# Gated mix of a spectral and a dense branch: output product 7 split a second time, product 3 on one couple less, some sums and partial results by DMA

## The chip, the core and the metric

The kernel runs on one core of a Trainium2 chip. The metric is the device time of one execution in microseconds (us). A core has five engines that each work through a queue of their own, in a fixed order: TensorE (PE in the profile; PEld is its weight load), VectorE (DVE), ScalarE (ACT), GpSimd (POOL) and SyncE (SP). Data move between DRAM and the on-chip buffer (SBUF) by DMA; matmuls write into PSUM banks.

## The reference

```python
# x 2048x1024, h 2048x3584, out 2048x1024, all fp32
a = x @ dft_hid_re.T ; b = x @ dft_hid_im.T
A = dft_seq_re @ a - dft_seq_im @ b          # real part of a 2-D DFT
h = relu(x @ w1 + b1) ** 2
B = h @ w2 + b2
g = sigmoid((x * gate_w).sum(-1, keepdims=True))
out = g * A + (1 - g) * B
```

## The kernel before

Nearly all the work is four big matrix products, in five parts. Part x makes a and b (the hidden DFT) and leaves them in DRAM as `ab`. Parts a and b make h from the first 2048 and the last 1536 columns of w1, and leave it in DRAM. Part c is the sequence DFT (with -Ci beside Cr its K is a and b together) and leaves the gated spectral branch in DRAM. Part o is h times w2, gated and added to that, and writes the output. The products of x, a and b are interleaved (constant `ORDER`); c and o follow, each in the order 1, 2, 5, 6, 3, 7, 4 of their products.

**Seven products.** A big product is split in 2 x 2 quarters and computed by seven products instead of eight (`FACTORS`): product p multiplies a quarter, or a sum of quarters, of the left side (S1 to S4) with one of the right side (T1 to T4), and the results are added up to the four quarters of the output. The class `Seven` (L422) keeps the partial results that several products share ("one", "u", "s", "v"). Those that the table `SPILL` names for a part are stored to DRAM (`keep`, L448) and, for the uses listed, read back by `get` (L458); the others stay in SBUF.

**A second level.** Inside a product the same is done once more where it is told to. For c and o (function `tall`, L617) K stands in 8 and 7 blocks, taken in couples of two. `TWICE_C` and `TWICE_O` say for each product how many couples are split into seven inner products; what is left of K is multiplied at one level. A couple takes 84 matmuls at two levels and 96 at one. A matmul has 128x128 weights and 512 columns (L1425).

**fp32 from three terms.** Each operand is split in a rounded part hi (ScalarE, L203, or L407 for a half-size one) and the rest lo (VectorE, L211 or L209, half-size L418 or L415); TensorE multiplies hi by hi, hi by lo and lo by hi. A half-size operand (256 columns) holds hi and lo in one tile, `both`. So every operand of every inner product costs ScalarE and VectorE a pass, and every sum of blocks one more (L182 at full size, L388 at half size), unless it is made by DMA.

**Sums by DMA.** `Side` (L333) makes the sums S and T of blocks. A sum that `BY_DMA` names for its side (`x_r` is the right side of part x, `o_r` of part o, and so on) isn't added on VectorE: SP loads one block, and POOL issues a DMA that adds the other to it (`accumulate`, L169). Plain loads are issued by SP, stores and adding DMAs by POOL.

**Inside a product at two levels** (`tall.product`). Inner products 1 and 6 share a group of PSUM banks, where `CHAIN` says so: 1 is emptied by ScalarE (`put`, L308: acc<-ps), 6 is then added on top. ScalarE empties also 5; VectorE adds (L321: acc+ps, L329: acc+acc) these to the four results so far. The second half, inner products 2, 3 and 4, starts from banks into which ScalarE loads a partial result (L255: ps<-acc). Which one that is, `LATE` decides:

```python
674:  late = old and p in LATE[name] and not ends
678:  f01, f11 = (both(old[b], f, 4, 0) if old and not late else f for b in (b01, b11))
680:  n01 = both(f01, t, 4, 0)
682:  n10 = both(old[b10], t, 4, 0) if old and not late else t
685:  onto = old if late else parts
686:  groups = {2: Group(2, [k2 + more], [onto[b00]]), 3: Group(2, [k2 + more], [onto[b01]]),
```

`old` is what the products before have left for the same quarter of the output. With `late` the banks are loaded with it, and the product's own inner results (`parts`) are added by VectorE when the second half is done; without, `old` and the inner results are first added on VectorE, and their sum is what the banks are loaded with. A finished quarter of part o is gated on VectorE (L960), the last ones row by row (L989).

**The order of the queues.** The kernel has a planner that runs when it is built: it holds a list of all operations with costs and due times, and plays them through to set a static order of each engine's queue, a slot of SBUF for each tile (55 slots) and a pair of PSUM banks for each group (4 pairs). `EARLY` puts the first sums of some sides ahead of time; `GUARD` bounds how far an engine may take work from further down while an operation of a PSUM bank is about to be ready (L1350, L1353); `DISTANT` holds operations back that are needed only much later, when few slots are free (L1358). So a change of one table can change the order on any engine.

Of the kernel before, what the change touches and what calls it, by code (L numbers as in the profile page):

```python
# [25 lines left out]
DMA_END = 2.2  # L26
GRID = 2.0

ORDER = (("ab", 1), ("x", 1), ("x", 2), ("b", 2), ("a", 2), ("b", 6), ("a", 6), ("x", 6), ("a", 5), ("b", 5), ("x",
         5), ("a", 3), ("x", 3), ("b", 3), ("a", 7), ("x", 7), ("b", 7), ("x", 4), ("a", 4), ("b", 4), ("c", 0), ("o",  # L30
         0))
ORDER_C = (1, 2, 5, 6, 3, 7, 4)
# [1 line left out]
INNER = {"x": (1, 5, 6, 3, 7, 2, 4), "a": (1, 5, 6, 3, 7, 2, 4), "b": (1, 5, 6, 3, 7, 2, 4)}  # L34
TWICE_X = (1, 2, 4, 5, 6, 7, 3)
TWICE_HA = (2, 3, 4, 5, 6, 7, 1)
TWICE_HB = (2, 3, 4, 5, 6, 7, 1)
TWICE_C = {1: 4, 2: 3, 3: 4, 4: 3, 6: 3, 5: 3}
TWICE_O = {1: 3, 2: 3, 3: 3, 4: 3, 6: 3}

FACTORS = {1: ((0, 0), (0, 0)), 2: ((0, 1), (1, 0)), 3: ("S4", (1, 1)), 4: ((1, 1), "T4"), 5: ("S1", "T1"),
           6: ("S2", "T2"), 7: ("S3", "T3")}
# [18 lines left out]
MIX_R = {"T1": ((0, 0), (0, 1), ADD), "T2": ((1, 1), "T1", SUB), "T3": ((0, 1), (1, 1), SUB),  # L61
         "T4": ("T2", (1, 0), ADD)}
LESS_X, LESS_H, LESS_C, LESS_O = (3, 4), (3, 4, 5), (2, 6), (3, 4, 5)
BY_DMA = {"x_l": ("S1", "S2", "S3", "S4"), "x_r": ("T4",), "h_l": ("S4",), "c_l": ("S1", "S2", "S3", "S4"), "c_r":
          ("T1", "T2", "T3", "T4"), "o_l": ("S3", "S4"), "o_r": ("T2", "T4")}

AHEAD = {"SP": 15.0, "POOL": 15.0, "ACT": 15.0, "DVE": 15.0}
FILL = {"DMA": 1.05, "ACT": 0.97, "DVE": 0.97}
# [4 lines left out]
KEEP = 5  # L73
EAGER = True
WARM = 38
LATE = {"c": (1, 2, 3, 4, 5, 6, 7), "o": (1, 2, 3, 4, 5, 6)}
DISTANT = (15.0, 6)
SPILL = {"one": ("", "x"), "u": ("xb", "ab"), "s": ("x", "xb"), "v": ("", "b")}
CHAIN = {"c": {1: 1, 2: 1, 3: 1, 4: 1, 5: 2, 6: 1, 7: 1}, "o": {3: 1, 1: 1, 2: 1, 4: 1, 6: 1, 7: 1}}
SUMMED = "xab"  # L80
ADD_S = ""
ADD_U = "bx"
EARLY = {"a_l": (("S2", "S1"), (), 90.0, 7.5), "b_l": (("S2",), (), 75.0, 15.0), "x_r": (("T1",), (), 60.0, 7.5)}
TOGETHER = True
OPEN = True
REST = 1.0
GUARD = (0.5, 1.0)
SOON = {"POOL": 12.0, "ACT": 6.0, "DVE": 6.0}
SLACK = {"SP": 3.0, "POOL": 2.0, "ACT": 0.6, "DVE": 0.6}
LEAD = {"SP": 3.0, "POOL": 1.0, "ACT": 2.0, "DVE": 2.0}  # L90
# [2 lines left out]
C_FORMS = ()  # L93
O_FORMS = ()
THROUGH_X = ("S1", "S2")
THROUGH_H = ("S2",)
THROUGH_W = ()
THROUGH_C = ("T2",)
THROUGH_O = ("T2",)
# [3 lines left out]
def gated_mix_kernel(ctx: ExitStack, tc: tile.TileContext, x4, xn, w4, ct, w1a, w1b, w2, b1, b2, gw, out):  # L103
# [201 lines left out]
    def put(group, seg, rp, scale=1.0, name="acc"):  # L305
        w, rows = Val(name), group.rows
        c, l = act(512 * min(2, rows - 2 * rp))
        group.take(seg, rp, Op("ACT", c, l, [], w, lambda: nc.scalar.activation(  # L308
            view(w.tile, rows, rp), view(group.ps[rp], rows, rp), AF.Copy, scale=scale)))
        return w  # L310
# [111 lines left out]
    class Seven:  # L422
# [97 lines left out]
    def wide(name, left, right, rows, second, less, final, from_ps, negative, flip, place=None):  # L520
# [13 lines left out]
        def product(p, old, quad):  # L534
# [37 lines left out]
            chain, other = Group(rows, [1] * 4), Group(rows, [1] * 2)  # L572
            opening = OPEN and name in ORDER[0][0] and p == (ALIKE[ORDER[0][1]] if name == "x" else ORDER[0][1])
            if opening:
# [42 lines left out]
    def tall(name, left, right, ksteps, order, second, less, final, from_ps, by_row=None):  # L617
# [4 lines left out]
        def product(p, old, quad):  # L622
# [26 lines left out]
            def block(q, j, c):  # L649
                if isinstance(r, str):  # L650
                    if (q, j, c) not in raw:
                        raw[q, j, c] = right[2 * q + j, c].of(r)
                    return raw[q, j, c]
                return right[2 * q + j, c].of(r)

            r2 = {q: Inner(lambda j, c, q=q: block(q, j, c), INNER_R) for q in range(k2)}
            chain = min(CHAIN[name].get(p, 0), k2)
            groups = {p2: Group(2, [k2]) for p2 in (1, 6, 7, 5) if p2 != 1 or not chain}
# [14 lines left out]
            ends = by_row and p == order[-1]  # L673
            late = old and p in LATE[name] and not ends
            t = put(g1, 0, 0)
# [97 lines left out]
    def order_of(run):  # L773
        return [ALIKE[p] if run == "x" and TOGETHER else p for r, p in ORDER if run in r]

    NEG = ((0, 1), (1, 0))

    def x_stage():
# [12 lines left out]
        def x_block(m, q):  # L791
            return lambda *k: Far(x4[2 * k[0] + m, k[1], q], 0.0) if len(k) > 1 else sum_of_x(m, q, k[0])

        keep = None if TOGETHER else lambda s, v, m, q: x_sums.__setitem__((m, q, s), (v, len(steps)))
        left = x_sides
        left.update({(m, q): Side(x_block(m, q), PLUS_L, BY_DMA["x_l"],
                                  keep=keep and (lambda s, v, m=m, q=q: keep(s, v, m, q)), through=THROUGH_X,
                                  made=had("x_l", (m, q)))
                     for m in range(2) for q in range(2)})
        right = {(q, c): Side(lambda j, n, q=q, c=c: Far(w4[n, c, j, q], 0.0), MIX_R, BY_DMA["x_r"], through=THROUGH_W,  # L800
                              made=had("x_r", (q, c)))
# [10 lines left out]
    def h_stage(part):  # L812
# [35 lines left out]
        def from_ps(quad, k, group, seg, rp):  # L848
            end(quad, k, None, lambda: group.ps[rp], lambda o: group.take(seg, rp, o))

        left = {(m, q): Side(lambda i, j, m=m, q=q: Far(w1[i, m, j, q], 0.0), MIX_L, BY_DMA["h_l"], rows * P,
                             through=THROUGH_H, made=had("ab"[part] + "_l", (m, q)))
                for m in range(2) for q in range(2)}
        names = {"T1": "S3", "T2": "S2", "T3": "S1", "T4": "S4"}

        def blocks(q, c):
            def get(*key):
                if len(key) == 1:
                    return sum_of_x(c, q, names[key[0]])
                j, n = key  # L860
                return Far(x4[2 * n + c, j, q], 0.0)
            return get
# [10 lines left out]
        right = {(q, c): Same(q, c) if TOGETHER else Side(blocks(q, c), None, ()) for q in range(2) for c in range(2)}  # L873
        return wide("ab"[part], left, right, rows, TWICE_HB if part else TWICE_HA, LESS_H, final, from_ps, False, True)

# [42 lines left out]
    def c_stage():  # L918
        rows = [Late(lambda n=n: row(n, 0, 1e9)) for n in range(2)]

        def end(quad, k, v, source, take=None):
# [14 lines left out]
            if take:  # L936
                take(o)
            store(gy[i, n, c, rp], w)

        left = {q: Side(lambda i, j, q=q: ab[j, q, i], PLUS_L, BY_DMA["c_l"], through=THROUGH_C,  # L940
                        made={f: c_forms[f, q] for f in C_FORMS}) for q in range(8)}
        right = {(q, c): Side(lambda j, n, q=q, c=c: Far(ct[n, c, j, q], 0.0), PLUS_R, BY_DMA["c_r"], through=THROUGH_C, made=had("c_r", (q, c)))
                 for q in range(8) for c in range(2)}
# [12 lines left out]
    def o_stage():  # L956
# [5 lines left out]
        def end(quad, k, v, source, take=None):  # L962
            (i, n), (c, rp) = quad, k
            r, y = rows[n, -1 if quad in NEG else 1].of(), gy[i, n, c, rp]
            w = Val("o")
            cc, l = dve(512)

            def first():
                for j in range(2):
                    begin(w.tile[:, j, :], source()[:, j, :], r.tile[:, c, :], 4 * i + 2 * rp + j, quad)  # L970

            o = Op("DVE", 2 * cc, cc + l, ([v] if v else []) + [r, b2v], w, first, over=[v] if v else [])
            o.soon = True
            if take:
                take(o)
            Op("POOL", 0.6, 2 * P * 4 * 512 * 2, [w, y], Far(y.at), lambda: nc.gpsimd.dma_start(y.at, w.tile, accum_op=ADD)
               ).twice = True

        def by_row(quad, k, group):
            (i, n), (c, rp) = quad, k  # L980
            r, y = rows[n, -1 if quad in NEG else 1].of(), load(gy[i, n, c, rp])
            for j in range(2):
# [3 lines left out]
                def emit(w=w, j=j):  # L986
# [7 lines left out]

        left = {q: Side(lambda i, j, q=q: Far(w2[i, j, q], 0.0), MIX_L, BY_DMA["o_l"], through=THROUGH_O, made=had("o_l", q)) for q in range(7)}
        right = {(q, c): Side(lambda j, n, q=q, c=c: h_far[j, q, 2 * n + c], PLUS_R, BY_DMA["o_r"], through=THROUGH_O,
                             made={f: o_forms[f, q, c] for f in O_FORMS})
                 for q in range(7) for c in range(2)}
        tall("o", left, right, 7, ORDER_O, TWICE_O, LESS_O, lambda quad, k, v: end(quad, k, v, lambda: v.tile),
             lambda quad, k, group, seg, rp: end(quad, k, None, lambda: group.ps[rp], lambda o: group.take(seg, rp, o)),  # L1000
# [4 lines left out]
    def sums_early():  # L1005
# [320 lines left out]
    def try_engine(e, now):  # L1326
# [6 lines left out]
        for o in queue:  # L1333
# [225 lines left out]
```

## Time and profile before

| | us |
|---|---|
| median of 3 runs | 1793.14 (1793.13 to 1793.51) |
| profiled execution, its own time | 1793.0 |
| span of the profile | 1791.1 |
| TensorE busy | 1785.1 (100%) |
| VectorE busy | 1621.8 (91%) |
| ScalarE busy | 1007.6 (56%) |
| GpSimd busy | 288.9 (16%) |

The parts follow one another in time: x, a and b from 5.4 to 738.5 us, c to 1293.4, o to the end. Part o's products 1, 2, 5, 6, 3, 7 and 4 end at 1361, 1429, 1506, 1574, 1642, 1718 and 1786 us. Times of matmuls start at the row's first number; TensorE is pipelined, so the time from start to start, and not a matmul's own length, is what one costs. Rows name instructions as out<-in with the kernel's names; "x2" means that the row stands for two of them, one behind the other. In brackets stands the idle time ahead of an instruction and what ended it.

### The profile page before, as it was taken

What the parts mean: (1) busy time and instruction counts of PE and PEld (TensorE: products, weight loads), DVE (VectorE), ACT (ScalarE), POOL (GpSimd) and SP (SyncE); (2) the same over time, 40 slices, a digit from 0 to 9 for tenths busy, and PEclk for the clock granted to TensorE, in tenths of its full rate; (3) what the DMA queues carried; (4) which work ended last, traced back from release to release, by engine and by line L of the source; (5) the groups of instructions that cost most, each with busy time, mean ns of one, the idle gap of its engine ahead of it and who ended that gap; (6) DMA issues with size and microseconds to landing.
All of it is one profiled execution on the core that took longest, in us unless ns stands there. A gap on an engine that the chain in (4) does not pass through costs nothing.

```text
span 1791.1 us, 21814 instructions
## 1 busy us (share of the span) xinstructions
PE 1785.1 (100%) x7892; PEld 1477.9 (83%) x7892; DVE 1621.8 (91%) x1671; ACT 1007.6 (56%) x1201; POOL 288.9 (16%) x416
## 2 busy tenths in 40 slices
PE   9999999999999999999999999999999999999998
PEld 8888888888888888888888888888888888888887
DVE  8896899999898897999998999559999998999887
ACT  7454743324669576866574747336476435754443
POOL 0113211011211222001133201202000031101020
PEclk9999999999999999999999999999999999999999
DMA  8959898898979999789899959999675997789992
GB/s 328 390 217 301 279 359 271 302 339 258 286 278 342 301 302 333 249 301 305 229 238 269 253 167 304 302 282 283 222 258 188 374 278 206 223 273 331 297 226 59
DMA packets 145531, 492.73 MB, mean 275 GB/s; under 512 B 15872, under 2 KB 29520, under 8 KB 145424
## 3 DMA queue, kind: packets, MB, share of 16 engines
q0 software_dynamic: 58064, 207.13, 44.2%
q1 hardware_dynamic: 86656, 283.04, 43.3%
q8 instruction: 62, 1.02, 0.2%
q10 hardware_dynamic: 704, 1.18, 0.2%
q14 instruction: 45, 0.37, 0.1%
HBM read 377.51 MB, written 113.78 MB: 274 GB/s over the span
## 4 chain that ended last, share of the span: by engine, by line
PE 99%; DMA 0%; DVE 0%; ACT 0%; issue 0%
PE ps L1425 99%; DMA raw<-in_x 0%; DVE o L960 0%; DVE o L989 0%; ACT hi L1464 0%
## 5 line engine op out<-in xcount | busy, mean ns | idle before, releaser
L1425 PE MATMUL ps<-hi 128*128 128x512 f32 x1638 | 635.9, 389 | 0.1
L1425 PE MATMUL ps<-hi,lo 128*128 128x512 f32 x1638 | 635.9, 389 | 0.0
L1425 PE MATMUL ps<-lo,hi 128*128 128x512 f32 x1638 | 635.7, 389 | 0.0
L1425 PE MATMUL ps<-hi,both 128*128 128x512 f32 x1960 | 605.2, 389 | 0.0
L203 ACT ACTIVATE hi<-raw 128x1024 fp32r<-128x1024 f32 (+1 forms) x326 | 333.2, 1038 | 269.5 <-DVE raw L182 183.1
L1425 PEld LDWEIGHTS ps<-hi,both 128*128 128x128 f32 x1960 | 367.9, 188 | 76.4
L211 DVE TENSOR_TENSOR lo<-raw,hi 128x1024 fp32r<-128x1024 f32 (+1 forms) x291 | 346.9, 1204 | 39.0 <-ACT hi L203 38.5
L1425 PE MATMUL ps<-lo,both 128*128 128x512 f32 x980 | 381.2, 389 | 0.0
L1425 PEld LDWEIGHTS ps<-hi,lo 128*128 128x128 f32 x1638 | 307.4, 188 | 64.3 <-DVE lo L211 0.4
L1425 PEld LDWEIGHTS ps<-hi 128*128 128x128 f32 x1638 | 307.4, 188 | 64.1 <-ACT hi L1464 0.4
L1425 PEld LDWEIGHTS ps<-lo,hi 128*128 128x128 f32 x1638 | 307.4, 188 | 63.9
L203 ACT ACTIVATE hi<-sum 128x1024 fp32r<-128x1024 f32 (+1 forms) x217 | 220.7, 1028 | 138.5 <-DVE sum L182 113.4
L211 DVE TENSOR_TENSOR lo<-sum,hi 128x1024 fp32r<-128x1024 f32 (+1 forms) x183 | 218.7, 1199 | 19.2 <-ACT hi L203 11.6
L321 DVE TENSOR_TENSOR acc<-acc,ps 128x1024 f32<-128x1024 f32 (+1 forms) x165 | 187.8, 1142 | 44.9 <-PE ps L1425 38.9
L1425 PEld LDWEIGHTS ps<-lo,both 128*128 128x128 f32 x980 | 183.9, 188 | 38.2
L308 ACT ACTIVATE acc<-ps 128x1024 f32<-128x1024 f32 (+1 forms) x135 | 132.9, 987 | 143.8 <-PE ps L1425 139.6
L182 DVE TENSOR_TENSOR raw<-raw 128x1024 f32<-128x1024 f32 (+1 forms) x146 | 168.3, 1173 | 0.0
L203 ACT ACTIVATE both<-sum 128x512 fp32r<-128x512 f32 x140 | 87.1, 624 | 86.5 <-DVE sum L388 59.0
L255 ACT ACTIVATE ps<-acc 128x1024 f32<-128x1024 f32 (+1 forms) x83 | 81.2, 980 | 73.6 <-DVE acc L321 66.4
L321 DVE TENSOR_TENSOR back<-back,ps 128x1024 f32<-128x1024 f32 x64 | 71.8, 1126 | 15.0 <-PE ps L1425 14.3
L407 ACT ACTIVATE both<-raw 128x512 fp32r<-128x512 f32 x105 | 64.7, 618 | 26.9 <-PE ps L1425 15.7
L182 DVE TENSOR_TENSOR sum<-sum 128x1024 f32<-128x1024 f32 (+1 forms) x56 | 65.6, 1181 | 9.6 <-DMA sum<-in_ct 6.3
(68 smaller groups left out, 1133.8 us busy)
## 6 DMA issues: line engine op xcount, KB each, us to landing
raw<-h SPq DMA_DIRECT2D x107, 512.0 KB, 6.3
raw<-in_ct SPq DMA_DIRECT2D x91, 512.0 KB, 7.6
raw<-in_w SPq DMA_DIRECT2D x81, 512.0 KB, 7.2
back<-v SPq DMA_DIRECT2D x48, 512.0 KB, 6.6
raw<-in_ct POOLq DMA_DIRECT2D x48, 512.0 KB, 12.3
raw<-ab SPq DMA_DIRECT2D x40, 512.0 KB, 11.3
t<-raw POOLq DMA_DIRECT2D x38, 512.0 KB, 12.2
sum<-t SPq DMA_DIRECT2D x38, 512.0 KB, 14.6
```

The costliest lines, as they stand in the source:

```text
L182: Op("DVE", c, l, [a, b], w, lambda: nc.vector.tensor_tensor(w.ap(), a.ap(), b.ap(), op=op), over=[a, b])
L203: nc.scalar.activation(self.hi()[:, k, :], src(v)[:, k, :], AF.Copy, scale=-1.0 if less else 1.0)
L211: nc.vector.tensor_tensor(a, b, c, op=SUB)
L255: lambda rp=rp, k=k, e=e, v=v: nc.scalar.activation(self.ps[rp][:, :k, :], v.tile[:, e:e + k, :], AF.Copy),
L308: group.take(seg, rp, Op("ACT", c, l, [], w, lambda: nc.scalar.activation(view(w.tile, rows, rp), view(group.ps[rp], rows, rp), AF.Copy, s ...
L321: nc.vector.tensor_tensor(a, b, d, op=ADD)
L407: Op("ACT", c, l, [v.base], hi, lambda: nc.scalar.activation(self.hi(), cols(v), AF.Copy, scale=-1.0 if less else 1.0), then=lambda t: set ...
L1425: nc.tensor.matmul(group.ps[r // group.per][:, r % group.per, :], a()[:, kk, r * P:(r + 1) * P], b()[:, kk, :], start=first and kk + n == ...
```

## The change

Only tables of the kernel change; no function is edited.

- Output product 7 is computed at two levels on three couples of K (it was at one level throughout), product 3 on two couples instead of three. `CHAIN` gets an entry for product 5 of o, which has no couple at two levels.
- The sums T1 of part x's right side (4 tiles) and T3 of part o's right side (14 tiles) are made by adding DMAs.
- `LATE` of part o loses 3 and 6. Product 7, now at two levels, is not in it either.
- `SPILL`: x's "one" is no longer stored and read back; the list of u has part a's first use in it, besides those of x and b, so all three parts read u back.
- Numbers of the planner: `ORDER` has a6 ahead of b6, `EARLY` and `GUARD` have other values, `DISTANT` holds nothing back any more. `THROUGH_H` and `TWICE_HB` alter no instruction.

```diff
-... ("b", 2), ("a", 2), ("b", 6), ("a", 6), ("x", 6), ...
+... ("b", 2), ("a", 2), ("a", 6), ("b", 6), ("x", 6), ...
-TWICE_HB = (2, 3, 4, 5, 6, 7, 1)
+TWICE_HB = (2, 4, 5, 6, 7, 1, 3)
 TWICE_C = {1: 4, 2: 3, 3: 4, 4: 3, 6: 3, 5: 3}
-TWICE_O = {1: 3, 2: 3, 3: 3, 4: 3, 6: 3}
+TWICE_O = {1: 3, 2: 3, 3: 2, 4: 3, 6: 3, 7: 3}
...
-BY_DMA = {... "x_r": ("T4",), ... "o_l": ("S3", "S4"), "o_r": ("T2", "T4")}
+BY_DMA = {... "x_r": ("T1", "T4"), ... "o_l": ("S3", "S4"), "o_r": ("T2", "T3", "T4")}
...
-LATE = {"c": (1, 2, 3, 4, 5, 6, 7), "o": (1, 2, 3, 4, 5, 6)}
-DISTANT = (15.0, 6)
-SPILL = {"one": ("", "x"), "u": ("xb", "ab"), "s": ("x", "xb"), "v": ("", "b")}
-CHAIN = {... "o": {3: 1, 1: 1, 2: 1, 4: 1, 6: 1, 7: 1}}
+LATE = {"c": (1, 2, 3, 4, 5, 6, 7), "o": (1, 2, 4, 5)}
+DISTANT = (1000.0, 0)
+SPILL = {"u": ("xab", "ab"), "s": ("x", "xb"), "v": ("", "b")}
+CHAIN = {... "o": {3: 1, 1: 1, 2: 1, 4: 1, 6: 1, 7: 1, 5: 1}}
...
-EARLY = {"a_l": (("S2", "S1"), (), 90.0, 7.5), ... "x_r": (("T1",), (), 60.0, 7.5)}
+EARLY = {"a_l": (("S2", "S1"), (), 70.0, 7.5), ... "x_r": (("T1",), (), 40.0, 7.5)}
...
-GUARD = (0.5, 1.0)
+GUARD = (0.7, 3.0)
```

The program has 7830 matmuls in its matrix products after the change, 7854 before; VectorE issues 25 instructions more, ScalarE 23 more, POOL 426 DMAs instead of 420, SP 547 instead of 562. At three places the new order of the queues is shown, with the numbers that tell tiles of one name apart.

**VectorE in product 4 of part x**, up to the lo that TensorE multiplies with at matmul 50 of that product. raw and sum are blocks and their sums, acc and back are partial results (back: one that was read back from DRAM), ps is a bank of PSUM. Before:

```order
L182 TENSOR_TENSOR raw_5109<-raw_5324,raw_5109 128x1024
L329 TENSOR_TENSOR back_5331<-back_5331,acc_5398 128x512
L321 TENSOR_TENSOR acc_5119<-acc_5119,ps_5377 128x1024
L321 TENSOR_TENSOR acc_5152<-acc_5152,ps_5400 128x1024
L209 SCALAR_TENSOR_TENSOR lo_5488<-sum_5407,hi_5442 128x1024
L329 TENSOR_TENSOR back_5361<-back_5361,acc_5413 128x1024
L182 TENSOR_TENSOR sum_5496<-sum_5288,sum_5401 128x1024
L211 TENSOR_TENSOR lo_5500<-sum_5401,hi_5409 128x1024
```

After:

```order
L182 TENSOR_TENSOR raw_5063<-raw_5296,raw_5063 128x1024
L329 TENSOR_TENSOR back_5322<-back_5322,acc_5391 128x512
L321 TENSOR_TENSOR acc_5110<-acc_5110,ps_5369 128x1024
L182 TENSOR_TENSOR sum_5449<-sum_5249,sum_5396 128x1024
L209 SCALAR_TENSOR_TENSOR lo_5477<-sum_5389,hi_5398 128x1024
L329 TENSOR_TENSOR back_5327<-back_5327,acc_5402 128x1024
L321 TENSOR_TENSOR acc_5145<-acc_5145,ps_5393 128x1024
L211 TENSOR_TENSOR lo_5492<-sum_5396,hi_5431 128x1024
```

The second addition out of PSUM (L321) and the sum of blocks (L182) have changed places.

**ScalarE in product 6 of part o**, from the row that empties a bank of inner product 1 to the second bank that is loaded. Before:

```order
L308 ACTIVATE acc_12736<-ps_12413 128x1024
L255 ACTIVATE ps_12713<-acc_11327 128x1024
L203 ACTIVATE hi_12744<-sum_12470 128x1024
L203 ACTIVATE hi_12760<-raw_11937 128x1024
L407 ACTIVATE both_12763<-raw_11946 128x2x256
L255 ACTIVATE ps_12738<-acc_11305 128x1024
```

After:

```order
L308 ACTIVATE acc_12742<-ps_12419 128x1024
L203 ACTIVATE both_12747<-sum_12415 128x2x256
L203 ACTIVATE hi_12764<-sum_12412 128x1024
L203 ACTIVATE hi_12767<-raw_11910 128x1024
L255 ACTIVATE ps_12720<-acc_11325 128x1024
L407 ACTIVATE both_12778<-raw_11942 128x2x256
L203 ACTIVATE hi_12793<-raw_11951 128x1024
L203 ACTIVATE both_12798<-sum_12506 128x2x256
L255 ACTIVATE ps_12744<-acc_11302 128x1024
```

The loads of the banks have moved back, behind three splits of operands (hi and both). In product 7, which had no second level before, **VectorE** now has these rows around the end of inner product 6; the acc on the left are the four results:

```order
L329 TENSOR_TENSOR acc_13042<-acc_13042,acc_13883 128x1024
L329 TENSOR_TENSOR acc_13072<-acc_13072,acc_13883 128x1024
L329 TENSOR_TENSOR acc_13042<-acc_13042,acc_13906 128x1024
L211 TENSOR_TENSOR both_13868<-sum_13559,both_13868 128x2x256
L321 TENSOR_TENSOR acc_13906<-acc_13906,ps_13620 128x1024
L211 TENSOR_TENSOR lo_13936<-sum_13538,hi_13888 128x1024
L329 TENSOR_TENSOR acc_13020<-acc_13020,acc_13906 128x1024
```

What the rows make are the sums that the banks of inner products 2, 3 and 4 are loaded with.

**ScalarE early in product 4 of part o**, up to the row that empties inner product 1's bank. Before:

```order
L203 ACTIVATE hi_14190<-sum_13837 128x1024
L203 ACTIVATE hi_14206<-sum_14188 128x1024
L203 ACTIVATE both_14214<-sum_14121 128x2x256
L203 ACTIVATE both_14232<-sum_14228 128x2x256
L308 ACTIVATE acc_14249<-ps_14118 128x1024
```

After:

```order
L203 ACTIVATE both_14231<-sum_14207 128x2x256
L203 ACTIVATE hi_14237<-sum_14186 128x1024
L203 ACTIVATE both_14271<-sum_14255 128x2x256
L203 ACTIVATE hi_14275<-sum_13813 128x1024
L308 ACTIVATE acc_14290<-ps_14163 128x1024
```

A full-size hi now stands just ahead of that row, where a half-size one stood.

More of the change, by code (lines that the diff above doesn't have):

```diff
@@ L27 @@
 GRID = 2.0
-ORDER = (("ab", 1), ("x", 1), ("x", 2), ("b", 2), ("a", 2), ("b", 6), ("a", 6), ("x", 6), ("a", 5), ("b", 5), ("x",
+ORDER = (("ab", 1), ("x", 1), ("x", 2), ("b", 2), ("a", 2), ("a", 6), ("b", 6), ("x", 6), ("a", 5), ("b", 5), ("x",
          5), ("a", 3), ("x", 3), ("b", 3), ("a", 7), ("x", 7), ("b", 7), ("x", 4), ("a", 4), ("b", 4), ("c", 0), ("o",
@@ L63 @@
 LESS_X, LESS_H, LESS_C, LESS_O = (3, 4), (3, 4, 5), (2, 6), (3, 4, 5)
-BY_DMA = {"x_l": ("S1", "S2", "S3", "S4"), "x_r": ("T4",), "h_l": ("S4",), "c_l": ("S1", "S2", "S3", "S4"), "c_r":
-          ("T1", "T2", "T3", "T4"), "o_l": ("S3", "S4"), "o_r": ("T2", "T4")}
+BY_DMA = {"x_l": ("S1", "S2", "S3", "S4"), "x_r": ("T1", "T4"), "h_l": ("S4",), "c_l": ("S1", "S2", "S3", "S4"),
+          "c_r": ("T1", "T2", "T3", "T4"), "o_l": ("S3", "S4"), "o_r": ("T2", "T3", "T4")}
 AHEAD = {"SP": 15.0, "POOL": 15.0, "ACT": 15.0, "DVE": 15.0}
@@ L75 @@
 WARM = 38
-LATE = {"c": (1, 2, 3, 4, 5, 6, 7), "o": (1, 2, 3, 4, 5, 6)}
-DISTANT = (15.0, 6)
-SPILL = {"one": ("", "x"), "u": ("xb", "ab"), "s": ("x", "xb"), "v": ("", "b")}
-CHAIN = {"c": {1: 1, 2: 1, 3: 1, 4: 1, 5: 2, 6: 1, 7: 1}, "o": {3: 1, 1: 1, 2: 1, 4: 1, 6: 1, 7: 1}}
+LATE = {"c": (1, 2, 3, 4, 5, 6, 7), "o": (1, 2, 4, 5)}
+DISTANT = (1000.0, 0)
+SPILL = {"u": ("xab", "ab"), "s": ("x", "xb"), "v": ("", "b")}
+CHAIN = {"c": {1: 1, 2: 1, 3: 1, 4: 1, 5: 2, 6: 1, 7: 1}, "o": {3: 1, 1: 1, 2: 1, 4: 1, 6: 1, 7: 1, 5: 1}}
 SUMMED = "xab"
@@ L82 @@
 ADD_U = "bx"
-EARLY = {"a_l": (("S2", "S1"), (), 90.0, 7.5), "b_l": (("S2",), (), 75.0, 15.0), "x_r": (("T1",), (), 60.0, 7.5)}
+EARLY = {"a_l": (("S2", "S1"), (), 70.0, 7.5), "b_l": (("S2",), (), 75.0, 15.0), "x_r": (("T1",), (), 40.0, 7.5)}
 TOGETHER = True
@@ L95 @@
 THROUGH_X = ("S1", "S2")
-THROUGH_H = ("S2",)
+THROUGH_H = ()
 THROUGH_W = ()
```

## The prediction

> **What bounds the kernel now.** I read the page's parts 1 and 2, then the chain of waits in order of time, then the timeline where TensorE stops, then the busy time product by product.
>
> ```profile
> span 1791.1 us, 21814 instructions
> PE 1785.1 (100%) x7892; PEld 1477.9 (83%) x7892; DVE 1621.8 (91%) x1671; ACT 1007.6 (56%) x1201; POOL 288.9 (16%) x416
> PEclk9999999999999999999999999999999999999999
> ...
> 5.42 1779.48 PE ps L1425 x7848
> ...
> 1784.93 0.76 DVE o L960
> ...
> 1787.10 0.69 DVE o L989
> ```
>
> TensorE works from 5.42 us to the end at its full clock; 5.4 us stand ahead of it and 6 behind, which no edit touches. 1779.48 us for 7848 matmuls are 226.7 ns each, start to start. The matmul groups of the page add up to 7854 (three of 1638, one of 1960, one of 980), so a whole stall of TensorE has room for about 0.3 us. It is in one place, 50 matmuls into x4 (product 4 of part x):
>
> ```profile
> 645.00 0.39 PE L1425 MATMUL ps<-lo,hi 128*128 128x512 f32 x1
> 645.35 0.50 PE L1425 MATMUL ps<-hi,lo 128*128 128x512 f32 x1
> 645.68 0.40 PE L1425 MATMUL ps<-hi 128*128 128x512 f32 x1
> ...
> 645.35 0.19 PEld L1425 LDWEIGHTS ps<-hi,lo 128*128 128x128 f32 x1 [0.39 <-DVE lo L211]
> ...
> 639.53 1.22 DVE L321 TENSOR_TENSOR acc<-acc,ps 128x1024 f32<-128x1024 f32 x1 [0.26 <-PE ps L1425]
> ...
> 644.08 1.22 DVE L211 TENSOR_TENSOR lo<-sum,hi 128x1024 fp32r<-128x1024 f32 x1
> ```
>
> Starts are 0.35 and 0.33 apart where 0.227 is normal: 0.12 waited for VectorE's lo (ended 645.30) and 0.11 to get going again, 0.23 in all. So every matmul counts in full, and VectorE, with hardly a gap of its own, is the next bound. By product of part o:
>
> ```profile
> core 0: us, PE busy (x) PEld busy (x) DVE busy (x) ACT busy (x) POOL busy (x), PEclk, DMA share, GB/s
> 1293.00:1361.00 68.00, 68.00 (x302) 56.31 (x301) 67.90 (x76) 44.22 (x54) 1.62 (x3) 1.00 0.59 209
> 1506.00:1574.00 68.00, 68.00 (x302) 56.31 (x301) 67.26 (x74) 45.30 (x56) 7.40 (x10) 1.00 0.60 172
> 1642.00:1718.00 76.00, 76.00 (x337) 62.94 (x336) 60.46 (x63) 32.21 (x35) 14.28 (x17) 1.00 1.01 281
> 1718.00:1786.00 68.00, 68.00 (x302) 56.17 (x300) 60.26 (x69) 33.07 (x40) 8.67 (x10) 1.00 0.58 121
> ```
>
> These are products 1, 6, 7 and 4. Two levels on three couples leave VectorE 0.1 to 0.7 us of 68 (products 1 and 6); product 7 at one level leaves 15.5 of 76, but there the DMA share is 1.01.
>
> **The change part by part.**
>
> *TWICE_O.* A couple of K takes 84 matmuls at two levels, 96 at one. Product 7 gains three couples, product 3 loses one: 24 matmuls less, 24 x 0.2267 = **-5.44 us**, all on the path. VectorE pays: the changed program has 43 full-size (1024) and 33 half-size instructions between product 7's first and last matmul, against 43 and 19. At the steps of the rows below (1.135 and 0.60 us from start to start) that is 68.6 us in a window of 68.0. It is product 1's load (67.90, no stall) and a little more; what covers it is the lead built up in product 3, which loses such work. I take 0 for throughput; the cover lacking entirely would be the 0.6.
>
> *The stall in x4.* VectorE's order ahead of that lo is shown with the change (the lo is the last row of both fences there). The same rows, but the second read of PSUM, which waited 0.26 us for TensorE, now stands three rows later, when its bank has long been ready. A stall of 0.12 goes with the 0.26: **-0.23 us**.
>
> *LATE without 3 and 6, and product 7 as it is built.* These now add the old partial result before the second half of the product: a bank is loaded (ScalarE, L255) only after VectorE's sum. The second pair of fences with the change shows product 6. Before, the load followed the emptying of the chain's bank at once; now it waits for VectorE's sums; the fence behind them shows how these are queued in product 7. The bank that its last row is loaded into is used 36 matmuls (8.16 us) after the end of inner product 6. Product 1, which has no old result, shows the nearest such chain and its prices:
>
> ```profile
> 1328.90 0.62 PE L1425 MATMUL ps<-hi,both 128*128 128x512 f32 x2
> ...
> 1323.89 1.03 ACT L308 ACTIVATE acc<-ps 128x1024 f32<-128x1024 f32 x1 [0.23 <-PE ps L1425]
> ...
> 1326.80 1.03 ACT L255 ACTIVATE ps<-acc 128x1024 f32<-128x1024 f32 x1
> 1328.19 1.03 ACT L255 ACTIVATE ps<-acc 128x1024 f32<-128x1024 f32 x1 [0.36 <-DVE acc L321]
> ...
> 1324.42 1.21 DVE L211 TENSOR_TENSOR lo<-raw,hi 128x1024 fp32r<-128x1024 f32 x1
> 1325.56 1.21 DVE L329 TENSOR_TENSOR acc<-acc 128x1024 f32<-128x1024 f32 x1
> 1326.87 1.22 DVE L321 TENSOR_TENSOR acc<-acc,ps 128x1024 f32<-128x1024 f32 x1
> 1328.01 0.68 DVE L418 TENSOR_TENSOR both<-raw,both 128x512 fp32r<-128x512 f32 x1
> 1328.61 1.22 DVE L182 TENSOR_TENSOR raw<-raw,sum 128x1024 f32<-128x1024 f32 x1
> ```
>
> There the first load ended at 1327.83, 1.30 us before its matmul (1329.13, the second of the first row). In product 7: three sums at 1.135, the half-size 0.60, two rows at 1.135, the last sum 1.22, 0.1 to hand over, the load 1.03 = 8.6 us, 0.46 late if the first sum begins just as inner product 6 ends. In product 6 a lo stands among the sums instead: 5.76 against 5.44 us (24 matmuls) for the first bank and again 8.6 against 8.16 for the second, 0.46 in all. Where in its row VectorE stands at that moment the order doesn't tell: half a row (0.57) either way gives 0 to 1.0 for each. I take 0.3 for each, nearer to the start on time; product 3 (two couples, 24 matmuls for a shorter chain) costs 0.
>
> *Behind product 7.* Its four results are added and gated on VectorE while product 4 starts. By the last pair of fences with the change, a hi that waits for VectorE's sum now stands just ahead of the row that empties inner product 1's bank, and TensorE needs that bank 12 matmuls (2.72 us) later. Prices:
>
> ```profile
> 1726.45 1.03 ACT L308 ACTIVATE acc<-ps 128x1024 f32<-128x1024 f32 x1 [0.77 <-PE ps L1425]
> 1727.50 1.06 ACT L203 ACTIVATE hi<-sum 128x1024 fp32r<-128x1024 f32 x1
> ...
> 1724.32 0.69 DVE L388 TENSOR_TENSOR sum<-raw 128x512 f32<-128x512 f32 x1
> 1724.93 1.41 DVE L960 SCALAR_TENSOR_TENSOR acc<-acc,b2c,g 128x512 f32<-128x512 f32 x2
> 1726.25 1.22 DVE L182 TENSOR_TENSOR sum<-sum 128x1024 f32<-128x1024 f32 x1
> ...
> 1728.74 0.61 PE L1425 MATMUL ps<-hi,both 128*128 128x512 f32 x2
> ```
>
> Before, the emptying ended at 1727.48, 1.49 ahead of its matmul (1728.97, the second of the two). After, VectorE has from product 7's end to that sum: the third result's add, a lo and the fourth's add (1.135 each), two gated pairs (1.32 each), two half-size rows (0.60), the sum 1.22 = 8.5 us, begun about 0.65 after that end (hand-over and half a row); hi (0.95) and emptying (1.03) follow, 11.15 us in, against 48 matmuls = 10.88. **0.3 late**, half a row either way: 0 to 0.9.
>
> Each of the four stops costs 0.11 more to restart, 0.44 (0, if none comes).
>
> *BY_DMA, SPILL.* Part o's 14 sums T3 and part x's 4 T1 leave VectorE (18 x 1.135 = 20.4 us, used up by the two levels) and become accumulates on POOL's queue; u of part a is read back once more (8 loads), x's "one" no longer stored and read. SP issues 15 DMAs fewer, POOL 6 more. What a pair of load and accumulate costs with both queues full, in part c (1140 to 1180), and what a load takes in part o (1506 to 1574):
>
> ```profile
> q0 software_dynamic: 1547, 5.65, 67.4%
> q1 hardware_dynamic: 1553, 5.66, 37.5%
> ...
> sum<-t SPq DMA_DIRECT2D x6, 512.0 KB, 30.4
> ...
> raw<-h SPq DMA_DIRECT2D x12, 512.0 KB, 5.0
> ```
>
> 5.66 MB are 10.8 loads and as many accumulates in 40 us: 3.7 us a pair, shares of 1.4 and 2.5 us. The program issues in products 6, 3, 7 now 16, 12, 15 accumulates and 27, 13, 24 plain ones: 43 x 2.5 + 64 x 1.4 = 197 us of 207; before 29 and 78, 182 of 212. It fits, the busiest being product 6 (78 us of 68 by the same prices), whose loads serve the products behind it. Cost 0, bounds 0 and what rival 3 says. [...]
>
> *The rest* (a6 ahead of b6, EARLY, GUARD, DISTANT) moves orders; the x4 place is where it shows. THROUGH_H and TWICE_HB alter no instruction. 0, unless a place that I haven't found is late.
>
> **Sum**, against the profiled execution's 1793.0: -5.44 - 0.23 + 0.3 + 0.3 + 0.3 + 0.44 = -4.3, 1788.7. The median of the runs is 0.14 above that execution: 1788.8.
>
> **Rivals.** (1) None of the chains is late: -5.67, 1787.5. For it: 0.3 us is a quarter of a row. Against: four places, each at its limit. (2) VectorE's lead is smaller than I take it; each place is a half to a whole row later, 3 to 6 us of stalls: 1790.5 to 1793. For it: 68.6 us of work in 68.0. (3) Slower: in product 6 the accumulates keep POOL's queue full, SP's loads land after 30 us instead of 5, and product 7's sums start late. Product 7 of before lived with a DMA share of 1.01, but VectorE had 15.5 us to spare there, now none: what is late beyond ScalarE's and VectorE's lead (some 10 us) stops TensorE, up to 15 us, 1803. It decides from 9.3 us of waiting (5.67 gained, 3.6 for 0.2%). Against: 197 of 207 us, and part c ran at that density without a stop.
>
> **How the numbers follow.** 0.2% (3.6 us) is about what a measurement of this kernel tells from no change; the bound is 1789.55. Forecast with 0.4 to 2.1 us of stalls (1787.9 to 1789.5): 0.67. Rival 1: 0.13. Rival 2: 0.14, within 0.2%. Rival 3: 0.06. Faster 0.80, same 0.14, slower 0.06. The range, from all of rival 1 to the near end of rival 2: 1787.2 to 1790.5.
>
> **What would show it.** 7830 matmuls; no stop at x4; ScalarE's L255 ending within 0.5 us of its matmul in o's products 6 and 7; its L308 late some 11 us into product 4. Wrong: idle TensorE behind a DMA, over 1 us at one place, or in parts x, a, b, c.

## The result, and the profile after

The changed kernel takes 1788.3 us (median of 9 runs, 1788.08 to 1790.2) against 1793.14 (9 runs, 1792.89 to 1793.54): a ratio of 0.9974, 95% interval 0.9964 to 0.9984. It is 4.8 us faster; forecast were 1788.8 and a range of 1787.2 to 1790.5. The profiled execution took 1788.53.

The head of the page of the changed kernel:

```profile
span 1786.7 us, 21834 instructions
PE 1780.1 (100%) x7868; PEld 1473.8 (82%) x7868; DVE 1637.1 (92%) x1696; ACT 1027.1 (57%) x1224; POOL 296.6 (17%) x422
```

From its chain of waits (start, us, what, in order of time) the rows of TensorE and of what it waited for last:

```profile
5.79 1669.49 PE ps L1425 x7362
...
1681.68 0.96 ACT hi L203
1682.64 1.02 ACT ps L255
...
1683.70 96.91 PE ps L1425 x426
```

TensorE has one gap that the chain takes for one, ahead of 1683.70, 168 matmuls into product 7, behind the load of a bank (L255). From the starts of the matmuls two smaller ones come out, both in product 6. The timeline of the changed kernel at the three (start, length, engine, line; in brackets idle time and releaser):

```profile
1541.15 0.79 PE L1425 MATMUL ps<-hi,both 128*128 128x512 f32 x2
...
1544.07 0.81 PE L1425 MATMUL ps<-hi,both 128*128 128x512 f32 x2
...
1683.04 0.39 PE L1425 MATMUL ps<-hi,both 128*128 128x512 f32 x1
1683.70 0.50 PE L1425 MATMUL ps<-hi,both 128*128 128x512 f32 x1 [0.28 <-ACT ps L255]
1684.05 0.40 PE L1425 MATMUL ps<-lo,both 128*128 128x512 f32 x1
...
1540.36 1.03 ACT L255 ACTIVATE ps<-acc 128x1024 f32<-128x1024 f32 x1 [0.78 <-DVE acc L329]
...
1543.31 1.01 ACT L255 ACTIVATE ps<-acc 128x1024 f32<-128x1024 f32 x1
...
1682.62 1.03 ACT L255 ACTIVATE ps<-acc 128x1024 f32<-128x1024 f32 x1
...
1675.03 3.49 DVE L329 TENSOR_TENSOR acc<-acc 128x1024 f32<-128x1024 f32 x3
...
1681.30 2.36 DVE L329 TENSOR_TENSOR acc<-acc 128x1024 f32<-128x1024 f32 x2
```

Product 7: the starts at 1683.04, 1683.70 and 1684.05 are 0.66 and 0.34 apart where 0.227 is normal, 0.44 late and 0.11 to restart. Product 6: the pair at 1544.07 is 0.31 apart, and the next 0.34, 0.08 + 0.11, behind the load that ends at 1544.32; its first load, which ends at 1541.39, holds up the pair at 1541.15 and costs 0.06 + 0.11. Together 0.91. The stop of 0.23 in x4 is gone, and there is none in product 4.

From profile to profile: -24 x 0.2267 - 0.23 + 0.91 = -4.76; TensorE also began 0.37 later (5.79 against 5.42), which leaves -4.39 of the measured -4.4 (span 1791.1 to 1786.7). That start lay anywhere from 5.3 to 5.8 in the profiles of all kernels below, and isn't part of the change; the medians, 4.84 apart, agree with -4.76. The readings are good to about 0.1: from TensorE's first matmul to its last the difference is 4.66, and 0.1 came off behind the last.

### The profile page after: what moved, and what is told of

It reads as the page before. It is cut to its first block, busy times and chain, and to the rows that moved or that the text cites. A ratio compares the mean times of both kernels' runs of the same rounds, so it can differ in the third digit from the quotient of the medians.

```text
span 1786.7 us, 21834 instructions
## 1 busy us (share of the span) xinstructions
PE 1780.1 (100%) x7868; PEld 1473.8 (82%) x7868; DVE 1637.1 (92%) x1696; ACT 1027.1 (57%) x1224; POOL 296.6 (17%) x422
## 4 chain that ended last, share of the span: by engine, by line
PE 99%; ACT 1%; DMA 0%; DVE 0%; issue 0%
PE ps L1425 99%; DMA raw<-in_x 0%; ACT hi L203 0%; ACT ps L255 0%; DVE o L960 0%; DVE o L989 0%; ACT both L407 0%; ACT acc L308 0%; ACT hi L1464 0%; ACT both L203 0%
## 5 line engine op out<-in xcount | busy, mean ns | idle before, releaser
L1425 PE MATMUL ps<-hi,both 128*128 128x512 f32 x2072 | 640.8, 389 | 0.3 <-ACT ps L255 0.3
L1425 PE MATMUL ps<-hi 128*128 128x512 f32 x1574 | 611.3, 389 | 0.5 <-ACT hi L1464 0.5
L1425 PE MATMUL ps<-lo,hi 128*128 128x512 f32 x1574 | 611.2, 389 | 0.0
L1425 PE MATMUL ps<-hi,lo 128*128 128x512 f32 x1574 | 611.2, 389 | 0.0
L1425 PEld LDWEIGHTS ps<-hi,both 128*128 128x128 f32 x2072 | 389.1, 188 | 82.0 <-ACT ps L255 1.4
L1425 PE MATMUL ps<-lo,both 128*128 128x512 f32 x1036 | 403.3, 389 | 0.0
L211 DVE TENSOR_TENSOR lo<-sum,hi 128x1024 fp32r<-128x1024 f32 (+1 forms) x195 | 235.2, 1211 | 6.2 <-ACT hi L203 3.7
L308 ACT ACTIVATE acc<-ps 128x1024 f32<-128x1024 f32 (+1 forms) x142 | 139.5, 987 | 123.9 <-PE ps L1425 118.8
L321 DVE TENSOR_TENSOR acc<-acc,ps 128x1024 f32<-128x1024 f32 (+1 forms) x152 | 172.5, 1140 | 39.9 <-PE ps L1425 38.1
L182 DVE TENSOR_TENSOR raw<-raw 128x1024 f32<-128x1024 f32 (+1 forms) x131 | 152.0, 1178 | 0.1
L255 ACT ACTIVATE ps<-acc 128x1024 f32<-128x1024 f32 (+1 forms) x83 | 81.2, 980 | 69.4 <-DVE acc L321 54.1
L321 DVE TENSOR_TENSOR back<-back,ps 128x1024 f32<-128x1024 f32 x64 | 71.9, 1129 | 14.8 <-PE ps L1425 14.3
L182 DVE TENSOR_TENSOR sum<-raw,sum 128x1024 f32<-128x1024 f32 (+1 forms) x65 | 77.8, 1197 | 1.0 <-PE ps L1425 0.9
```

The source lines that it names most:

```text
L182: Op("DVE", c, l, [a, b], w, lambda: nc.vector.tensor_tensor(w.ap(), a.ap(), b.ap(), op=op), over=[a, b])
L211: nc.vector.tensor_tensor(a, b, c, op=SUB)
L255: lambda rp=rp, k=k, e=e, v=v: nc.scalar.activation(self.ps[rp][:, :k, :], v.tile[:, e:e + k, :], AF.Copy),
L321: nc.vector.tensor_tensor(a, b, d, op=ADD)
L1425: nc.tensor.matmul(group.ps[r // group.per][:, r % group.per, :], a()[:, kk, r * P:(r + 1) * P], b()[:, kk, :], start=first and kk + n == ...
```

## The experiments

Stops below are read as above, from the starts of matmuls; each run is compared with the kernel before on the same chip, whose median was 1793.17 to 1793.19.

**The second level alone, and what it needs.** Three kernels start from the one before and add one edit after the other.

```diff
-TWICE_O = {1: 3, 2: 3, 3: 3, 4: 3, 6: 3}
+TWICE_O = {1: 3, 2: 3, 3: 2, 4: 3, 6: 3, 7: 3}
```

> The kernel before with the new TWICE_O and nothing else (7830 matmuls). Theory, VectorE is the next bound: product 7 has 68.6 us of VectorE work and the 14 sums T3 (14 x 1.135 = 15.9 us) for a window of 68.0. Of the 16.5 us too many, some 10 are covered if they can be made ahead, none if not, so TensorE stops 6 to 16 us, in product 7 at the loads of its banks above all: 1793.1 - 5.4 + (6 to 16) = 1794 to 1804. Rival, the lead of the products before covers them: 1787.7 to 1789, and the sums by DMA were not needed.

1817.1 us, ratio 1.0132 (1.0117 to 1.0147): 24 us slower, beyond the range that the theory gave. The stops sum to 13.1 us in product 7, the slow restart included, but also to 7.1 in product 1 and 2.8 in c, which the edit does not name: the planner sets the whole order anew. What TensorE waits for most in this kernel (us, times, longest):

```profile
PE ps L1425 <- ACT ps L255: 12.8, 2, 7.8
PE ps L1425 <- DVE acc L321: 2.5, 2, 1.8
PE ps L1425 <- DVE lo L211: 1.8, 2, 1.6
```

The stretch from 1293 to 1361 of it, nearly all of which is product 1 (1297 to 1372; us, then busy time of PE, PEld, DVE, ACT, POOL, granted clock, DMA share, GB/s):

```profile
1293.00:1361.00 68.00, 63.02 (x271) 51.70 (x270) 68.00 (x75) 42.55 (x53) 2.18 (x4) 0.95 0.58 212
```

VectorE is busy for 68.00 of 68, the DMA share is 0.58, and the bank loads that wait for its sums hold TensorE up. VectorE is the limit; the rival falls.

```diff
-"o_r": ("T2", "T4")
+"o_r": ("T2", "T3", "T4")
```

> The kernel before with the new TWICE_O and T3 of part o by DMA; LATE, SPILL, T1 and the planner's numbers stay. Theory, the two edits hold the whole gain and LATE only costs: the stop in x4 stays (0.23), product 6 has none, product 7 about 0.55: 1793.1 - 5.44 + 0.55 = 1788.2. Rival, LATE is worth something: with 3 and 6 in LATE the additions of their old results come after the second half of each product and reach into product 7, where a bank's load is then late by several rows of 1.135 us: 1790.5 or more, in one stop in product 7.

1793.58 us, 1.0003 (0.9994 to 1.0012). The sums by DMA bring 23.5 us back, and still nothing is gained: one stop in product 7 takes 6.1 us, at the same matmul 168. The rival is right in the amount; how it comes about shows in VectorE's own waits in products 6 and 3 of this kernel:

```profile
DVE acc L321 <- PE ps L1425: 7.5, 2, 5.2
```

and in its timeline, in the row that ends the longest of them:

```profile
1630.86 0.69 DVE L418 TENSOR_TENSOR both<-raw,both 128x512 fp32r<-128x512 f32 x1
1636.80 1.22 DVE L321 TENSOR_TENSOR acc<-acc,ps 128x1024 f32<-128x1024 f32 x1 [5.25 <-PE ps L1425]
```

With 3 and 6 in LATE, VectorE adds out of PSUM when the second half of the product is done. Such a row stands in VectorE's fixed order and waits for TensorE, and nothing behind it goes ahead: 7.5 us of VectorE's time are lost just ahead of the product that has none to spare. The waits came with the sums by DMA. With T3 still on VectorE, in the kernel of the run before, the same row for products 6 and 3 (1516.6 to 1659.9) is

```profile
DVE acc L321 <- PE ps L1425: 0.9, 1, 0.9
```

and in the kernel before the change (1506 to 1642)

```profile
DVE acc L321 <- PE ps L1425: 1.0, 1, 1.0
```

```diff
-"o": (1, 2, 3, 4, 5, 6)
+"o": (1, 2, 4, 5)
```

> As the run before it, and LATE of part o without 3 and 6. Theory, LATE only costs: product 6 has its two stops (0.36) beside product 7's 0.55 and x4's 0.23: 1788.6, slower than without. Rival, LATE pays: back to about 1788.3 from 1790.5 or more.

1788.27 us, 0.9972 (0.9961 to 0.9983): with three edits the whole gain is there. VectorE's waits in products 6 and 3 of this kernel:

```profile
DVE o L960 <- PE ps L1425: 3.5, 1, 3.5
DVE lo L211 <- ACT hi L203: 1.0, 1, 1.0
DVE acc L321 <- PE ps L1425: 0.4, 1, 0.4
```

The 7.5 us on L321 have become 0.4: ScalarE (L308) now empties those banks, and VectorE's additions need only what is in SBUF. In all VectorE idles 4.9 us there instead of 9.9 (3.5 of the 4.9 at the gating of a finished quarter, L960), and the stop in product 7 is 0.43 instead of 6.1. The theory that LATE only costs is wrong in sign. It was also wrong in place: in this order product 6 has no stop at all.

> The kernel before with LATE of part o without 3 and 6, nothing else (7854 matmuls). Theory, LATE moves additions forward in time and makes VectorE's lead larger, which is worth something only where product 7 needs it; alone it costs the two stops in product 6: 1793.5. Rival, it helps by itself too: 1793.0 or less. Second rival, without T3 by DMA the sums ahead of product 6's bank loads are later still: 1 to 3 us in product 6, 1794.5 to 1796.

The edit is the LATE line above, alone. 1795.51 us, 1.0013 (1.0003 to 1.0022): a stop of 1.90 us in product 6, by the second rival. The same edit costs 2.3 us by itself and is worth 5.3 on top of the two others. No one of the three can be given a price of its own. T3 by DMA alone, and TWICE_O with LATE but without T3, were not run.

**The knobs around it.**

```diff
-EARLY = {"a_l": (("S2", "S1"), (), 70.0, 7.5), ... "x_r": (("T1",), (), 40.0, 7.5)}
+EARLY = {"a_l": (("S2", "S1"), (), 90.0, 7.5), ... "x_r": (("T1",), (), 60.0, 7.5)}
-SPILL = {"u": ("xab", "ab"), ...}
+SPILL = {"one": ("", "x"), "u": ("xb", "ab"), ...}
-"x_r": ("T1", "T4")
+"x_r": ("T4",)
```

> The changed kernel with EARLY, SPILL and T1 of part x as before. Theory, as predicted these cost and give nothing: 1788.3, the same three stops in o's products 6 and 7, none in x, a and b. Rival, T1 by DMA is needed in part x: 4 x 1.135 = 4.5 us more VectorE work there shows as stops in x's products: up to 1792.8.

1788.7 us, 0.9974 (0.9964 to 0.9984), with the same three stops to the hundredth (0.06 + 0.11, 0.08 + 0.11, 0.44 + 0.11) and none in x, a and b. EARLY, partial results through DRAM and T1 by DMA in part x neither cost nor give anything that shows: the medians are 0.4 us apart, and no stop is different.

```diff
-DISTANT = (1000.0, 0)
+DISTANT = (15.0, 6)
```

> The changed kernel with DISTANT as before, (15, 6). Theory, the exchange of two rows of VectorE in x4 comes from the order of a6 and b6 or from EARLY and GUARD, and DISTANT does nothing: 1788.3 with no stop in x4. Rival, DISTANT holds back what a6 needs first, now that a6 stands ahead of b6: a stop of some us in a6, 1790 to 1795, and x4's stop of 0.23 back.

1796.32 us, 1.0016 (1.0006 to 1.0025). The rival is right twice, though the time is 1.3 us above its range. The stop in x4 is back (0.38), so it was DISTANT, and none of the others tried, that took it away; and 24 matmuls into a6 TensorE stands still. From the timeline of this kernel:

```profile
220.62 0.39 PE L1425 MATMUL ps<-hi,lo 128*128 128x512 f32 x1
225.74 0.80 PE L1425 MATMUL ps<-hi 128*128 128x512 f32 x1 [4.73 <-ACT hi L203]
227.00 0.79 PE L1425 MATMUL ps<-lo,hi 128*128 128x512 f32 x1 [0.46 <-DVE lo L211]
...
223.32 1.22 DVE L182 TENSOR_TENSOR sum<-raw 128x1024 f32<-128x1024 f32 x1
224.57 1.23 DVE L182 TENSOR_TENSOR sum<-sum,raw 128x1024 f32<-128x1024 f32 x1
```

VectorE begins the sums behind that operand only at 223.32 us, 2.5 us after TensorE's next matmul was due (220.85). All of it costs 8.2 us in a6, the slow restart included (below).

```diff
-... ("b", 2), ("a", 2), ("a", 6), ("b", 6), ...
+... ("b", 2), ("a", 2), ("b", 6), ("a", 6), ...
```

> The changed kernel with ORDER as before (b6 ahead of a6). Theory, only DISTANT and the x4 rows are tied together and ORDER does nothing: 1788.3, no stop in x, a or b. Rival, with DISTANT off the order of a6 and b6 decides what VectorE does early: a stop of about 1 us in the products a2, a6 or b6, 1789.2.

1789.27 us, 0.9978 (0.9969 to 0.9987): one stop of 0.98 in a2, by the rival, which had 1789.2; none in x4. So ORDER and DISTANT belong together: DISTANT off clears x4, and ORDER keeps that from costing 1 us in a2. GUARD was not tried alone.

```diff
-"o": (1, 2, 4, 5)
+"o": (1, 2, 4, 5, 6, 7)
```

> The changed kernel with 6 and 7 in LATE of part o as well (3 stays out). Theory, the stops in products 6 and 7 are bank loads behind VectorE's sums; with LATE the banks are loaded with the old result and both go (-0.91), but product 7's additions now come with product 4's: 0.5 to 1.5 us of stops in product 4, 1787.9 to 1788.9. Rival, 6 in LATE takes VectorE's lead away again: 3 us or more in product 7, over 1790.

1789.28 us, 0.9978 (0.9969 to 0.9987). The stop in product 7 is gone, and so are the two at product 6's bank loads, so those stops were the bank loads behind VectorE's sums. In their place product 4 has 1.38, where it waits for a lo of VectorE, and product 3 has 0.16; two new stops of 0.1 stand 49 matmuls into product 6 and in the first products of a and b. The mechanism is the theory's; the time is 0.4 us above its range (1.75 of stops against 0.91 is +0.84, measured +1.0).

**How much room the DMA engines had.** Behind every adding DMA of T3, one copy of 512 KB in DRAM, then two:

```diff
+        def emit():
             nc.gpsimd.dma_start(w.ap(), src.at, accum_op=ADD)
+            for f in spare:
+                nc.gpsimd.dma_start(f.at, src.at)
```

> The changed kernel, every queue in the same order, with one more DMA behind each of the 14 adding DMAs of T3 in part o: a copy of 512 KB from DRAM to DRAM on POOL's queue, whose result nobody reads. By the prices of the prediction 14 x 1.4 = 20 us of transfers are added to the 197 us of products 6, 3 and 7, 217 for a time of 205. Theory of rival 3, the DMA engines are at their limit there: some of the blocks and sums come late and TensorE stops 2 to 10 us behind DMAs in products 6, 7 or 4: 1790 to 1798. Other theory, the transfers are far enough ahead (15 us): 1788.3.

1794.77 us, 1.0007 (0.9997 to 1.0016): 6.5 us more than the changed kernel, and its gain is used up. Stops of 3.0 in product 7 and 4.3 in product 4, where the emptying of a bank (L308 there, L315 in this kernel, whose lines stand 7 to 8 lower) is late, the place that the prediction had for 0.3.

> The same with two copies behind each: 236 us of transfers for 205, 31 too many against a lead of some 10 to 15. Theory of rival 3: 15 to 20 us of stops, 1803 to 1808. Other theory, the sum of prices overstates the load by a tenth or more: under 1798.

1808.8 us, 1.0089 (1.0074 to 1.0104), a little above the range that rival 3's theory gave: 18 us of stops in product 7, 9.6 of them at its first matmul, and 5.9 in product 4, slow restarts included. VectorE waits for a block ahead of product 7 in this kernel:

```profile
1647.29 1.23 DVE L189 TENSOR_TENSOR raw<-raw 128x1024 f32<-128x1024 f32 x1 [2.47 <-DMA raw<-h]
```

So the limit was near. Busy tenths of the DMA engines from 1506 to 1720 us in 40 slices of 5.35 us, and SP's loads of h with the median time to landing, in the changed kernel:

```profile
DMA  0199999999999999999999730899999999999999
...
raw<-h SPq DMA_DIRECT2D x30, 512.0 KB, 13.5
```

and with 14 copies:

```profile
DMA  0299999999999999999999999599999999999999
...
raw<-h SPq DMA_DIRECT2D x30, 512.0 KB, 18.0
```

The changed kernel's engines rest once, from 1624 to 1645, for some 11 us (0.3, 0.7, 1.0 and 0.2 of slices). The 14 copies fill most of that pause; of their 20 us (the estimate of 14 x 1.4) some 9 are left, and 6.5 arrive as stops. In the kernel before such a load landed after 6.6 us in the same stretch, with 28 copies after 22.7. The copies also stand in POOL's own queue between the adding DMAs, so these two runs do not tell a full queue of POOL from full DMA engines; that SP's loads land later as well says that the engines have a part in it.

**One couple more.** The runs said that VectorE is the limit and that sums by DMA pay for couples while the DMA engines have a pause. Product 5 has T1 on its right side, and its window is the longest:

```diff
-TWICE_O = {... 7: 3}
+TWICE_O = {... 7: 3, 5: 1}
-"o_r": ("T2", "T3", "T4")
+"o_r": ("T1", "T2", "T3", "T4")
-DISTANT = (1000.0, 0)
+DISTANT = (15.0, 4)
-ROOM, TAKE = 53, 5.0
+ROOM, TAKE = 52, 6.0
```

> The changed kernel with one couple of output product 5 at two levels as well (7818 matmuls), T1 of part o by DMA too, and three of the planner's numbers: DISTANT (15, 4), ROOM 52 instead of 53, TAKE 6 instead of 5. Theory, VectorE's work is the limit and each group of sums that leaves it pays a couple: 14 x 1.135 = 15.9 us leave, one couple's operands come, and 12 matmuls x 0.2267 = 2.72 us go; if the three stops of the changed kernel (0.91) go with the new order, 1788.3 - 2.7 - 0.9 = 1784.7, else 1785.6. Rival, the DMA engines: the 14 sums T1 make 14 plain loads into adding DMAs, 14 x 1.1 = 15 us more of transfers, and where the copies stopped TensorE these do too: 1787 to 1792.

1785.17 us, 0.9956 (0.9943 to 0.9968): faster than both, 3.1 us less than the changed kernel. Stops: 0.36 in x4, 0.09 in product 6, none in products 7 and 4. By its parts -36 x 0.2267 - 0.23 + 0.45 = -7.94, measured -8.0. Two stretches of this kernel, the first over product 5 (1430 to 1503), the second over most of product 7 (1642 to 1710), columns as above:

```profile
1429.00:1506.00 77.00, 77.00 (x342) 63.77 (x341) 69.50 (x71) 36.99 (x40) 22.84 (x30) 1.00 1.04 261
...
1645.00:1713.00 68.00, 68.00 (x301) 56.31 (x300) 68.00 (x77) 45.98 (x56) 14.74 (x18) 1.00 1.05 299
```

The DMA share is 1.04 over product 5, and the transfers still come in time; the rival falls.

> The same with T1 of part o on VectorE as in the changed kernel. Theory, VectorE's work is the limit: 15.9 us more of it ahead of and in product 5, of which some 10 are covered; 2.7 us gained, 6 to 16 lost, and more by the slow restart behind a long stop: 1792 to 1802, with stops at the bank loads of part o's products. Rival, product 5's window (76 us with 48.5 of one-level work) has room for them: 1785 to 1786.

The same without the second of the four edits. 1801.32 us, 1.0048 (1.0034 to 1.0062): 16 us for 14 sums, 6.8 of it in a stop in product 1, 5.3 in product 6, 3.7 in c. TensorE's waits in this kernel:

```profile
PE ps L1425 <- ACT ps L255: 8.4, 2, 5.0
PE ps L1425 <- DVE lo L211: 1.6, 2, 1.4
```

As in the first run, sums put back on VectorE stop TensorE at bank loads, also well ahead of the product that they belong to (product 1 and part c) and behind it (product 6).

## Why the prediction was right, and where it was wrong

- **The 24 matmuls, -5.44**: right; all of them came off the path.
- **The stop in x4, -0.23**: right in size; the reason given holds in part. The second read of PSUM no longer waits ahead of that lo, as these rows of the changed kernel show, without an idle time:

```profile
642.14 1.23 DVE L321 TENSOR_TENSOR acc<-acc,ps 128x1024 f32<-128x1024 f32 x1
643.27 1.23 DVE L211 TENSOR_TENSOR lo<-sum,hi 128x1024 fp32r<-128x1024 f32 x1
```

  But the lo ends 1.1 us ahead of its matmul (645.59), and the wait was worth 0.26: VectorE had already come 0.8 us further, measured against TensorE, before it reached these rows. With DISTANT back the lo is 0.27 late and no such wait stands ahead of it. So what DISTANT, which the runs name as the edit, changes is how far VectorE has come by then; the prediction left open which edit it was.
- **Bank loads in product 6 and 7, 0.3 each and 0.11 per restart**: they measured 0.36 for the two places in product 6 and 0.55 in product 7, 0.91 against 0.93 (0.6 and three restarts). That the two agree so closely is luck: without the restarts product 6's loads were 0.14 late and product 7's 0.44, for 0.3 each, and the errors cancel. In product 7 the first sum began at 1675.03, just as inner product 6 ended (36 matmuls, 8.16 us, ahead of the late one at 1683.27), and the load ended 8.6 us later at 1683.65: the working held, and only the phase, half a row either way, had been a guess.
- **The emptying in product 4, 0.3 late**: wrong, 0.36 early. From the timeline of the changed kernel:

```profile
1722.35 1.06 ACT L203 ACTIVATE hi<-sum 128x1024 fp32r<-128x1024 f32 x1 [0.56 <-DVE sum L182]
1723.31 1.01 ACT L308 ACTIVATE acc<-ps 128x1024 f32<-128x1024 f32 x1
...
1724.45 0.62 PE L1425 MATMUL ps<-hi,both 128*128 128x512 f32 x2
...
1713.75 1.24 DVE L329 TENSOR_TENSOR acc<-acc 128x1024 f32<-128x1024 f32 x1
...
1721.01 1.24 DVE L182 TENSOR_TENSOR sum<-sum 128x1024 f32<-128x1024 f32 x1
```

  The emptying ends at 1724.32, the matmul is due at 1724.68. The chain is as long as forecast (1713.75 to 1722.25, 8.5 us), but the step "begun about 0.65 after that end" was wrong: the third result's addition does not wait for the bank that product 7 finishes last, so VectorE reached it 0.05 ahead of product 4's first matmul (1713.80). This stop and its restart, 0.41 us, are most of the 0.5 by which the forecast was too slow.
- **Throughput, 0**: right in time, but "the cover lacking entirely would be the 0.6" put the stake far too low. VectorE worked 67.97 of 68 us in product 7 of the changed kernel. Everything on VectorE's path has to be there: TWICE_O by itself is 24 us slower than before, and with the sums by DMA but without LATE 5.3 us are missing.
- **LATE, a cost**: wrong in sign. The prediction counted what leaves VectorE's order later (the bank loads) and did not look at what no longer stands in it: rows that wait for a bank of TensorE at the end of products 6 and 3. These waits are hardly there before (1.0 us): they grow to 7.5 when T3's sums leave VectorE, which then reaches such rows ahead of TensorE. The sum came out because it was made for all the edits together; that LATE supplied the cover which the prediction credited to product 3 is luck.
- **The transfers, 0**: right, and rival 3 did not come. Its point of decision was nearer than the 6% chance sounds: an estimated 20 us of transfers more use the gain up, 40 make the kernel 0.9% slower. The sum of 197 of 207 us was itself some 5% high: its prices, 2.5 and 1.4, add up to 3.9 for a pair that was measured at 3.7, since the shares of the two queues add up to 105%.
- **The rest, 0**: right for the set. Single edits of it are worth 1 us (ORDER) and 8 us (DISTANT) once the others are there.
- Rival 1 (1787.5) needed no late chain, rival 2 stops of 3 us or more; with 0.91 of stops the forecast's own case held.

## What to carry to other kernels

An engine with a fixed order loses time at every row that waits, also for everything behind that row (VectorE 5.25 us at one addition here); where such an engine is about to become the bound, look first for rows of it that wait for the bound of today, and let an engine with room do them. Tables that set one plan have prices together, not one by one: undo them in the order in which they need each other before calling one of them useless. Sums by adding DMAs are a real trade of VectorE's time for transfers (the 14 of T3 brought 23.5 us back), here as long as the transfers had a pause left to fill. The waits to look for can come with the relief itself: in products 6 and 3 they went from 0.9 to 7.5 us when VectorE was given less to do.

## What the runs showed of the hardware that was not expected

A long stop of TensorE cost more than its length in these runs. Around the stop in product 7 of the kernel with TWICE_O and T3, ahead of it and behind it (columns as above; the clock is the number ahead of the DMA share):

```profile
1678.00:1682.60 4.60, 4.60 (x22) 3.80 (x21) 4.60 (x6) 4.60 (x7) 0.85 (x1) 1.00 1.05 273
...
1688.50:1690.50 2.00, 2.00 (x6) 1.52 (x6) 2.00 (x3) 0.00 (x0) 0.00 (x0) 0.50 1.06 277
```

The granted clock fell to 0.50, matmuls started 0.427 us apart instead of 0.227 for about 3.5 us, and the stop of 4.41 us cost 6.1. At four stops in three kernels the addition is the same: 4.41, 5.13, 3.60 and 2.58 us of stop cost 1.69, 1.68, 1.71 and 1.71 more. It is not a constant: 5.14 us cost 1.91 in the kernel with TWICE_O alone, and with 28 copies 4.39, 7.10 and 4.37 us cost 1.51, 2.51 and 3.00, since the matmuls behind them ran at the slow rate for 3 to 6 us. The shortest, in product 4 of the kernel with 14 copies, with a granted clock of 0.50 from 1730.3 to 1733.0, by its timeline:

```profile
1726.85 0.39 PE L1433 MATMUL ps<-hi,both 128*128 128x512 f32 x1
1729.66 0.50 PE L1433 MATMUL ps<-hi,both 128*128 128x512 f32 x1 [2.42 <-ACT acc L315]
```

The stops of 1.55 and 1.20 us in product 7 of that kernel cost 0.11 each to restart: behind them the starts are 0.34 apart once (1682.07 to 1682.41, 1686.13 to 1686.47) and then 0.23 again. Other single stops, of up to 1.95 us, cost 0.1 as well; one of 1.79 with another of 0.38 right behind it, in product 7 of the kernel with TWICE_O alone, was followed by slow matmuls too.
